# Borders between blocks of 768 tokens: preparation ahead of the last second products, weight remainders in halves, two PSUM banks exchanged in every second pair

## The chip, the cores and the metric

The kernel runs on one core of one Trainium2 chip, in one launch. The metric is device time in microseconds, from three runs before the change (median 1062.34, lowest 1061.27, highest 1062.95). A core has five engines with a queue of instructions each: PE (TensorE, matrix products; its weight loads are listed as PEld), DVE (VectorE), ACT (ScalarE), POOL (GpSimd) and SP, which here only issues DMA transfers. They run side by side and wait for each other by semaphores.

## The reference

The program chains three parts. An attention with a position bias gives 2304 tokens of 512 values. Two feed-forward layers follow, each with two products (512 to 2048 and 2048 to 512):

```python
def _moe_ref(x, w_in, w_out):
    h = x @ w_in
    g = h - np.tanh(h)
    return (g @ w_out).astype(np.float32)

def _moe2_ref(x, w_in, w_out, s, b):
    h = x @ w_in
    r = np.maximum(h, 0.0)
    g = s * (r * r) + b
    return (g @ w_out).astype(np.float32)
```

The change concerns the second of them (layer 1) alone.

## The kernel before

All products keep float32 accuracy by splitting a matrix into a rounded part and a remainder (`rounded`, `rest`, line 92); a product is then three matmuls: high by high, high by low, low by high.

The attention and the first layer come first, up to about 666 us. The second layer works on three blocks of 768 tokens (`SUPER`, the loop over `q`), one after the other. A block has three stages.

**Eight pairs.** The loop over `p` takes two of the 16 groups of hidden units at a time, for both halves (384 tokens) of the block. It uses a seven-product scheme in place of eight block products (a Strassen-Winograd scheme): `combine` (line 644) forms four sums of weight quarters on POOL in tile XB, and `part` (line 652) splits weights and sums into a rounded part (three copies on ACT) and a remainder (line 92, three subtractions on POOL), in tile `C0` or `C1` by turns. `product` (line 824) is six matmuls of 384 columns. A pair has seven products in four PSUM banks X, Y, Z, V: first X, Y, Z, V, then X, Z, V again. ACT and DVE add them up, apply the squared ReLU (`squashed`, L718, and `units`, L722) and, for the first half of the tokens, split the result with `upper` (L728, ACT) and `lower` (L734, DVE). For the second half the two results of each pair are kept whole in SBUF, as "held units". Between the products of a pair stand the second products of the pair before, for half 0 (`second_products`, line 582: per hidden group 3 token tiles with three matmuls of 512 columns).

**The border.** After the last pair the second products of half 0 for hidden groups 14 and 15 are due, then `leave` (L586) copies the three accumulated tiles out, one on DVE and two on ACT.

**Half 1.** For each of the 16 held units, `ahead(f)` allots two buffers of a ring of 11 (tag "bias") and calls `upper` and `lower`; `second_products(1, f)` then does nine matmuls with them into banks Z, V and a3. The ring is also used by `leave` and by the pairs.

In the same loop the next block's tokens are prepared: `tokens(q + 1)` returns 15 steps, kept in the list `xq`: two loads, then rounding copies on ACT (`hi`, L679) and remainders and differences on DVE (`lo`, L682, and `minus`, L685, both of them with two inputs from SBUF). Three steps are taken at the end of the last pair, the fourth behind the preparation of unit 1, the others one per unit. The last block has no successor: it has none of this, and leaves its last three units' products to be ordered by token tile.

The order of every engine's queue is the order of the program; there is no planner that reorders. Around the border the program has this order (lines 894 to 907):

```python
            ahead(0)
            second_products(0, NF - 2, pend.pop(0))
            ahead(1)
            if xq:
                xq.pop(0)()
            second_products(0, NF - 1, pend.pop(0))
            if not final:
                part(q + 1, 0)
                combine(q + 1, 1)
            late = 3 if final else 0
            for f in range(NF - late):
                ahead(f + 2)
                if xq:
                    xq.pop(0)()
                second_products(1, f, gs.pop(f))
```

The opening of a block is its first pair, `p` = 0, and the first four products of `p` = 1. In the first block the last second products of layer 0 lie between them (`fill`); in the other two blocks nothing does, so the eleven products follow each other directly.

Of the kernel before, what the change touches and what calls it, by code (L numbers as in the profile page):

```python
# [24 lines left out]
NF = DFF // 128  # L25
# [35 lines left out]
def tile_kernel(ctx, tc, qk, vd, wcat, wts, sb, ltab, psib, ipsi8, out):  # L61
# [8 lines left out]
    def place(tag, shape, dtype=F32):  # L70
        return pools[0 if tag in EARLY else 1].tile([128] + shape, dtype, tag=tag, name=tag)
# [19 lines left out]
    def rest(lo, raw, hi):  # L91
        nc.gpsimd.tensor_tensor(out=lo, in0=raw, in1=hi.bitcast(F32), op=ALU.subtract)  # L92
# [118 lines left out]
    with ExitStack() as c0:  # L211
# [40 lines left out]
        for n in range(NG + 2):  # L252
# [18 lines left out]
            if n < NG:  # L271
# [3 lines left out]
                f = 512 - y  # L275
# [23 lines left out]
    def ring(dtype):  # L299
        return bp.tile([128, S], dtype, tag="bias", name="ring")  # L300
# [59 lines left out]
    with ExitStack() as ca:  # L360
# [163 lines left out]
        for n in range(NK + 6):  # L524
# [30 lines left out]
            if n in TK:  # L555
                k, j = TK[n]
# [11 lines left out]
    with ExitStack() as cb:  # L568
# [5 lines left out]
        def accumulate(layer, o, w, gh, gl, d, first, last):  # L574
            if layer == 0:
                wh, wl_ = (w[:, l, d * 128:d * 128 + 128] for l in range(2))
                prods = ((wh, gh), (wh, gl), (wl_, gh))
            else:
                a, l = gh[:, d * 128:d * 128 + 128], gl[:, d * 128:d * 128 + 128]
                prods = ((a, w[:, 0]), (a, w[:, 1]), (l, w[:, 0]))  # L580
            for j, (x, y) in enumerate(prods):
                nc.tensor.matmul(o, x, y, start=first and j == 0, stop=last and j == 2)  # L582
# [63 lines left out]
        def part(q, p):  # L646
            w, sums_ = wf_t.pop((q, p)), sums_at.pop((q, p))
            cs = cs_t[q, p] = place(f"C{(p + q) % 2}", [7, 2, 256], F32R)
            groups = ((slice(4, 6), w[:, 0].rearrange("p (o n) -> p o n", o=2)), (slice(6, 7), w[:, 1:2, 256:512]),
                      (slice(0, 4), sums_))  # L650
            for o, x in groups:
                nc.scalar.copy(cs[:, o, 0], x)  # L652
            for o, x in groups:
                rest(cs[:, o, 1], x, cs[:, o, 0])

        def unit(u, i, l):
            k = (0, 4, 6, 2, 8, 10, 12)[u] + i
            tag, k0 = ("XA", 0) if k < 4 else ("C2", 4) if k < 9 else ("C3", 9)
            if tag not in unit_at:
                unit_at[tag] = place(tag, [4 if k0 == 0 else 5, 2, 384], F32R)  # L660
            return unit_at[tag][:, k - k0, l]
# [55 lines left out]
        def squashed(layer, c, t):  # L717
            nc.scalar.activation(out=t, in_=c, func=(AF.Tanh, AF.Relu)[layer])  # L718
# [29 lines left out]
        xq = tokens(0)  # L748
        for n in range(NS):
# [15 lines left out]
            c, f = seq[n]  # L765
# [33 lines left out]
        def bank(t, n=384):  # L799
            return (ps_a if t[0] == "a" else ps_g).tile([128, 512], F32, tag=t, name=t)[:, 0:n]  # L800

        fill = [lambda: gemm2(*seq[-2]), lambda: gemm2(*seq[-1])]
        for q, (layer, s_) in enumerate(SUPER):
            nd = 3 if layer else 4
            cols = 512 if layer else 384
            c0 = s_ * 768
            final = q == len(SUPER) - 1
            accs = {}
            g_at.clear()

            def second_products(half, f, gs):
                order = (["a0", "a1", "a2", "a3"], ["V", "Y", "Z", "X"] if not layer else ["Z", "V", "a3"])[half][:nd]
                for d in range(nd):
                    if f == 0:
                        accs[half, d] = bank(order[d], cols)
                    accumulate(layer, accs[half, d], wt[f, 1], *gs, d, f == 0, f == NF - 1)
                    if f == NF - 1:
                        leave(accs[half, d], layer, d, c0 + half * 384)

            def product(o, p, a, u, begins):  # L820
                cs = cs_t[q, p]
                for i in range(2):
                    for j, (l, r) in enumerate(((0, 0), (0, 1), (1, 0))):
                        nc.tensor.matmul(o, cs[:, a, l, i * 128:i * 128 + 128], unit(u, i, r),  # L824
                                         start=begins and i == 0 and j == 0, stop=i == 1 and j == 2,
                                         skip_group_check=not begins)

            pend = []
            for p in range(NF // 2):
                X, Y, Z, V = (bank(t) for t in "XYZV")  # L830
                load_w(q, p + 2)
                u2, r, t_x = (ring(F32)[:, 0:384] for _ in range(3))
                product(X, p, 4, 0, True)
                nc.scalar.copy(u2, X)
                if p + 1 < NF // 2:
                    part(q, p + 1)
                product(Y, p, 0, 1, True)
                nc.vector.tensor_tensor(out=u2, in0=Y, in1=u2, op=ALU.add)
                product(Z, p, 1, 2, True)
                nc.vector.tensor_tensor(out=r, in0=Z, in1=u2, op=ALU.add)  # L840
                product(V, p, 2, 3, True)
                nc.vector.tensor_tensor(out=Y, in0=V, in1=r, op=ALU.add)
                if pend:
                    second_products(0, 2 * p - 2, pend.pop(0))
                elif fill:
                    fill.pop(0)()
                squashed(layer, Y, r)
                units(layer, held_unit(2 * p + 1), Y, r)
                product(X, p, 5, 4, False)
                squashed(layer, X, t_x)  # L850
                units(layer, X, X, t_x)
                product(Z, p, 6, 5, False)
                nc.vector.tensor_tensor(out=Z, in0=Z, in1=u2, op=ALU.add)
                g1 = two()
                upper(layer, X, g1)
                t_z = ring(F32)[:, 0:384]
                squashed(layer, Z, t_z)
                lower(layer, X, g1)
                units(layer, Z, Z, t_z)
                product(V, p, 3, 6, False)  # L860
                nc.vector.tensor_tensor(out=V, in0=V, in1=u2, op=ALU.add)
                g2 = two()
                upper(layer, Z, g2)
                lower(layer, Z, g2)
                squashed(layer, V, t_z)
                units(layer, held_unit(2 * p), V, t_z)
                if pend:
                    second_products(0, 2 * p - 1, pend.pop(0))
                elif fill:
                    fill.pop(0)()  # L870
                pend = [g1, g2]
                if p + 1 < NF // 2:
                    combine(q, p + 2)
                if q == 0 and p == 0 and layer:
                    renewed(NF - 3)
                    for f in (NF - 2, NF - 1):
                        renew(f)
                if q == 0 and p == 1 and layer:
                    for f in (NF - 2, NF - 1):
                        renewed(f)  # L880

                if p == NF // 2 - 1 and not final:
                    xq = tokens(q + 1)
                    for _ in range(3):
                        xq.pop(0)()
            gs = {}

            def ahead(f):
                if f < NF:
                    gs[f] = two()  # L890
                    upper(layer, held_unit(f), gs[f])
                    lower(layer, held_unit(f), gs[f])

            ahead(0)
            second_products(0, NF - 2, pend.pop(0))
            ahead(1)
            if xq:
                xq.pop(0)()
            second_products(0, NF - 1, pend.pop(0))
            if not final:  # L900
                part(q + 1, 0)
                combine(q + 1, 1)
            late = 3 if final else 0
            for f in range(NF - late):
                ahead(f + 2)
                if xq:
                    xq.pop(0)()
                second_products(1, f, gs.pop(f))
            if late:
                ahead(NF - 1)  # L910
                for d in range(nd):
                    for f in range(NF - late, NF):
                        accumulate(layer, accs[1, d], wt[f, 1], *gs[f], d, False, f == NF - 1)
                    r0 = c0 + 384 + d * 128
                    o = ring(F32)[:, 0:512]
                    for h, copy, queue in ((slice(0, 256), nc.scalar.copy, nc.scalar), (slice(256, 512), nc.vector.tensor_copy, nc.sync)):
                        copy(o[:, h], accs[1, d][:, h])
                        queue.dma_start(out=out[r0:r0 + 128, h], in_=o[:, h])
# [57 lines left out]
```

## Time and profile before

| | us |
|---|---|
| median of three runs | 1062.34 |
| the profiled execution, its own time | 1059.94 |
| its span | 1058.2 |
| PE busy | 1042.2 |
| DVE busy | 626.9 |
| ACT busy | 535.3 |
| POOL busy | 459.7 |

The span runs from the first to the last instruction of one profiled execution; times within it are counted from its start. Rows of a timeline give a start, a duration, the engine, the line and operation, what is written and read, how many instructions are merged into the row, and in brackets the idle time just before with the instruction that ended it. Instructions of one engine overlap a little, so that the distance from start to start is shorter than a duration. In the kernel before, the first border's half 1 begins at 764.06 us and the second block's first pair at 800.06.

### The profile page before, as it was taken

What the parts mean: (1) busy time and instruction counts of PE and PEld (TensorE: products, weight loads), DVE (VectorE), ACT (ScalarE), POOL (GpSimd) and SP (SyncE); (2) the same over time, 40 slices, a digit from 0 to 9 for tenths busy, and PEclk for the clock granted to TensorE, in tenths of its full rate; (3) what the DMA queues carried; (4) which work ended last, traced back from release to release, by engine and by line L of the source; (5) the groups of instructions that cost most, each with busy time, mean ns of one, the idle gap of its engine ahead of it and who ended that gap; (6) DMA issues with size and microseconds to landing.
All of it is one profiled execution on the core that took longest, in us unless ns stands there. A gap on an engine that the chain in (4) does not pass through costs nothing.

```text
span 1058.2 us, 19045 instructions
## 1 busy us (share of the span) xinstructions
PE 1042.2 (98%) x7048; PEld 844.0 (80%) x7048; DVE 626.9 (59%) x1297; ACT 535.3 (51%) x1110; POOL 459.7 (43%) x630
## 2 busy tenths in 40 slices
PE   9999999999999999999999999999999999999998
PEld 6566666666688888899888888999878998799986
DVE  8888888888577555533544325555575556655552
ACT  8987787877465433323332334554444444444441
POOL 0067777787468312130131062575225662166500
PEclk9999999999999999999999999999999999999999
DMA  8957464542264164330542331311302122022000
GB/s 286 326 167 275 154 220 162 180 135 91 105 258 140 67 206 149 126 120 31 195 164 80 124 106 52 113 45 41 110 0 91 41 60 90 0 90 60 2 30 30
DMA packets 53772, 124.87 MB, mean 118 GB/s; under 512 B 6064, under 2 KB 12336, under 8 KB 53680
## 3 DMA queue, kind: packets, MB, share of 16 engines
q1 hardware_dynamic: 53248, 123.28, 34.8%
q8 instruction: 55, 0.90, 0.3%
q10 hardware_dynamic: 432, 0.39, 0.1%
q14 instruction: 37, 0.30, 0.1%
HBM read 90.19 MB, written 33.46 MB: 117 GB/s over the span
## 4 chain that ended last, share of the span: by engine, by line
PE 87%; DVE 4%; POOL 2%; ACT 1%; issue 1%; DVEq 0%; POOLq 0%; ACTq 0%
PE a L582 31%; PE h L340 19%; PE o L504 7%; PE s L405 6%; PE X L824 5%; PE V L824 5%; PE Z L824 5%; PE t L449 3%; PE Z L582 3%; PE V L582 2%; PE Y L824 2%; POOL pn L443 1%; DVE raw L412 1%; DVE XA L682 1%; PE c L449 1%
## 5 line engine op out<-in xcount | busy, mean ns | idle before, releaser
L582 PE MATMUL a<-ring,w 128*128 128x512 f32 (+1 forms) x960 | 210.3, 368 | 0.0
L582 PEld LDWEIGHTS a<-ring,w 128*128 128x128 f32 x960 | 168.4, 189 | 29.8
L443 POOL TENSOR_SCALAR pn<-p,sm 128x576 f32<-128x576 f32 (+2 forms) x224 | 131.7, 604 | 40.8 <-DVE sm L434 35.5
L582 PE MATMUL a<-w,ring 128*128 128x512 f32 x576 | 146.6, 392 | 0.0
L349 DVE TENSOR_TENSOR h<-h,ring 128x512 f32<-128x512 f32 (+1 forms) x80 | 51.7, 646 | 152.1 <-ACT ring L348 152.0
L348 ACT ACTIVATE ring<-h 128x512 f32<-128x512 f32 (+1 forms) x80 | 44.4, 555 | 187.0 <-PE h L340 187.0
L582 PEld LDWEIGHTS a<-w,ring 128*128 128x128 f32 x576 | 107.6, 188 | 20.5
L340 PE MATMUL h<-X,C 128*128 128x512 f32 (+1 forms) x576 | 118.3, 355 | 0.0
L92 POOL TENSOR_TENSOR C<-st,C 128x512 fp32r<-128x512 f32 (+1 forms) x48 | 47.9, 1020 | 159.2 <-ACT C L652 105.7
L412 DVE CUSTOM_DVE_ANT_0 raw<-s,bias 128x576 f32<-128x576 f32 x144 | 103.9, 753 | 19.0 <-PE s L405 14.5
L426 ACT ACTIVATE p<-raw,mn 128x576 f32<-128x576 f32 x144 | 110.9, 774 | 7.1 <-DVE mn L412 4.3
L340 PEld LDWEIGHTS h<-X,C 128*128 128x128 f32 x576 | 96.3, 189 | 16.3 <-issue 0.8
L504 PE MATMUL o<-pt,vv 128*64 128x256 f32 (+1 forms) x640 | 95.0, 418 | 1.3 <-DVE xo L511 1.3
L405 PE MATMUL s<-qk 64*128 64x288 f32 (+1 forms) x640 | 91.8, 430 | 1.7 <-DVE mn L412 1.3
L136 POOL TENSOR_SCALAR s<-st 128x512 f32<-128x512 f32 x36 | 23.3, 649 | 150.7 <-DMA st<-in_wts 115.0
L405 PEld LDWEIGHTS s<-qk 64*128 64x128 f32 (+1 forms) x640 | 47.0, 175 | 42.6 <-DVE mn L412 18.6
L357 DVE TENSOR_TENSOR ring<-h,ring 128x512 fp32r<-128x512 f32 (+1 forms) x80 | 50.9, 637 | 43.6 <-ACT ring L356 39.2
L340 PE MATMUL h<-XA,C 128*128 128x512 f32 x288 | 70.6, 390 | 0.0
L340 PEld LDWEIGHTS h<-XA,C 128*128 128x128 f32 x288 | 53.9, 188 | 11.0
L356 ACT CAST ring<-h 128x512 fp32r<-128x512 f32 (+1 forms) x80 | 43.5, 543 | 36.5 <-DVE h L349 36.5
L487 ACT COPY pt<-t 128x512 f32<-128x512 f32 x64 | 37.4, 584 | 43.8 <-PE c L449 26.9
L449 PEld LDWEIGHTS t<-ident,pn 64*128 64x128 f32 x1184 | 51.8, 139 | 9.6 <-DVE pt L487 1.5
(118 smaller groups left out, 1854.0 us busy)
## 6 DMA issues: line engine op xcount, KB each, us to landing
st<-in_wts SPq DMA_DIRECT2D x36, 512.0 KB, 3.7
w<-in_wts SPq DMA_DIRECT2D x28, 512.0 KB, 5.0
qk<-in_qk SPq DMA_DIRECT2D x16, 864.0 KB, 5.5
st<-w_d SPq DMA_DIRECT2D x24, 512.0 KB, 3.5
bias_d<-m SPq DMA_DIRECT2D x36, 296.0 KB, 4.6
bias<-bias_d SPq DMA_DIRECT2D x32, 288.0 KB, 4.2
w_d<-s SPq DMA_DIRECT2D x32, 256.0 KB, 2.1
vv<-in_vd SPq DMA_DIRECT2D x16, 320.0 KB, 3.7
```

The source lines that it names most:

```text
L92: nc.gpsimd.tensor_tensor(out=lo, in0=raw, in1=hi.bitcast(F32), op=ALU.subtract)
L340: nc.tensor.matmul(h, a, x, start=(k == 0), stop=(k == 3 * KD - 1))
L349: nc.vector.tensor_tensor(out=h, in0=h, in1=t, op=(ALU.subtract, ALU.mult)[layer])
L357: nc.vector.tensor_tensor(out=gl, in0=g, in1=gh.bitcast(F32), op=ALU.subtract)
L405: nc.tensor.matmul(o[0:n, c, 0:288], q[h, ee, t * 128:t * 128 + n], kk[h, ee], start=True, stop=True)
L412: nc.vector.tensor_tensor_reduce(out=raw.rearrange("p (c j) -> p c j", c=2), in0=s_t.pop((x, j))[:, :, 0:288], in1=bias_t[pairs[i][0], k]. ...
L426: nc.scalar.activation(out=p, in_=raw, func=AF.Exp, scale=-1.0, bias=mn, accum_out=sm[:, j:j + 1])
L443: nc.gpsimd.tensor_scalar(out=pn[:, c:c + b - a], in0=p[:, a:b], scalar1=sm[:, j:j + 1], scalar2=0.0, op0=ALU.mult, op1=ALU.add)
L449: nc.tensor.transpose(out_, in_, ident[ROWS[r], ROWS[r]])
L504: nc.tensor.matmul(o[h], v[:, e, j], unit_t[i, u][:, 8 if j == 4 else 4 * e + j, 0:n], start=(j == 0), stop=(j == 4))
L582: nc.tensor.matmul(o, x, y, start=first and j == 0, stop=last and j == 2)
L824: nc.tensor.matmul(o, cs[:, a, l, i * 128:i * 128 + 128], unit(u, i, r), start=begins and i == 0 and j == 0, stop=i == 1 and j == 2, skip_ ...
```

## The change

`part` no longer subtracts the four sums' remainders in one instruction of 1024 columns but in two of 512. In pairs with an odd number the names X and Y stand for each other's bank. At the border the order is new: unit 0, then `part` of the next block's first pair, then unit 1, the second products of group 14, unit 2, those of group 15, then `combine`. In half 1 the loop prepares unit f+3 instead of f+2, and the token steps begin with unit 1 instead of between units 1 and 2 of the preparation.

```diff
-            for o, x in groups:
+            for o, x in groups[:2]:
                 rest(cs[:, o, 1], x, cs[:, o, 0])
+            for k in (0, 2):
+                rest(cs[:, k:k + 2, 1], sums_[:, k:k + 2], cs[:, k:k + 2, 0])
...
-                X, Y, Z, V = (bank(t) for t in "XYZV")
+                X, Y, Z, V = (bank(t) for t in ("XYZV", "YXZV")[p % 2])
...
             ahead(0)
+            if not final:
+                part(q + 1, 0)
+            ahead(1)
             second_products(0, NF - 2, pend.pop(0))
-            ahead(1)
-            if xq:
-                xq.pop(0)()
+            ahead(2)
             second_products(0, NF - 1, pend.pop(0))
             if not final:
-                part(q + 1, 0)
                 combine(q + 1, 1)
             late = 3 if final else 0
             for f in range(NF - late):
-                ahead(f + 2)
-                if xq:
+                ahead(f + 3)
+                if f and xq:
                     xq.pop(0)()
                 second_products(1, f, gs.pop(f))
             if late:
-                ahead(NF - 1)
```

## Rows read from the trace of the kernel before

**Rows 1.** The page, part 1: busy us, share of the span, instructions

```profile
PE 1042.2 (98%) x7048; PEld 844.0 (80%) x7048; DVE 626.9 (59%) x1297; ACT 535.3 (51%) x1110; POOL 459.7 (43%) x630
```

**Rows 2.** The waits of PE from 600 us on: us in total, times, longest

```profile
PE Z L582 <- ACT ring L728: 4.6, 2, 2.3
PE X L824 <- DVE ring L734: 1.0, 2, 0.5
```

**Rows 3.** Stages (length; PE, PEld, DVE, ACT, POOL busy; clock; DMA): border, opening, border

```profile
757.90:800.06 42.16, 39.82 (x173) 31.78 (x172) 26.58 (x45) 19.09 (x39) 8.21 (x7) 1.00 0.05 19
800.06:812.32 12.26, 11.74 (x68) 11.42 (x67) 7.86 (x14) 7.52 (x15) 9.01 (x9) 1.00 0.48 152
...
886.50:928.66 42.16, 39.79 (x173) 31.79 (x172) 26.59 (x45) 19.09 (x39) 8.21 (x7) 1.00 0.05 20
```

**Rows 4.** Timeline of PE, last border: its first group and its last

```profile
1015.10 6.32 PE L582 MATMUL a<-w,ring 128*128 128x512 f32 x27
...
1051.86 2.20 PE L582 MATMUL a<-w,ring 128*128 128x512 f32 x9
```

**Rows 5.** Timeline of PE, first border: half 1's start and its unit 3

```profile
764.06 0.84 PE L582 MATMUL Z<-w,ring 128*128 128x512 f32 x3
...
769.50 0.84 PE L582 MATMUL a<-w,ring 128*128 128x512 f32 x3
772.62 1.15 PE L582 MATMUL Z<-w,ring 128*128 128x512 f32 x3 [2.29 <-ACT ring L728]
```

**Rows 6.** Timeline of ACT, first border

```profile
760.73 1.12 ACT L728 ACTIVATE ring<-X,sb_t 128x384 fp32r<-128x384 f32 x2
...
764.74 0.93 ACT L652 CAST C<-st 128x512 fp32r<-128x512 f32 x2
765.57 1.05 ACT L652 CAST C<-XB 128x1024 fp32r<-128x1024 f32 x1
766.51 0.62 ACT L728 ACTIVATE ring<-X,sb_t 128x384 fp32r<-128x384 f32 x1
...
771.54 0.51 ACT L679 CAST XA<-C 128x384 fp32r<-128x384 f32 x1 [4.01 <-DVE C L685]
771.96 1.12 ACT L728 ACTIVATE ring<-X,sb_t 128x384 fp32r<-128x384 f32 x2
```

**Rows 7.** Timeline of DVE, first border

```profile
761.38 1.15 DVE L734 SCALAR_TENSOR_TENSOR ring<-X,sb_t,ring 128x384 fp32r<-128x384 f32 x2 [0.62 <-ACT ring L728]
762.44 0.55 DVE L682 TENSOR_TENSOR XA<-C,XA 128x384 fp32r<-128x384 f32 x1
...
767.77 2.74 DVE L682 TENSOR_TENSOR XA<-C,XA 128x384 fp32r<-128x384 f32 x1
...
775.15 1.02 DVE L685 TENSOR_TENSOR C<-C 128x384 f32<-128x384 f32 x2
777.26 0.62 DVE L734 SCALAR_TENSOR_TENSOR ring<-X,sb_t,ring 128x384 fp32r<-128x384 f32 x1 [1.10 <-ACT ring L728]
```

**Rows 8.** Timeline of POOL, first border

```profile
765.44 2.00 POOL L92 TENSOR_TENSOR C<-st,C 128x512 fp32r<-128x512 f32 x2 [18.74 <-ACT C L652]
767.39 2.71 POOL L92 TENSOR_TENSOR C<-XB,C 128x1024 fp32r<-128x1024 f32 x1
770.17 0.92 POOL L644 TENSOR_TENSOR XB<-st 128x256 f32<-128x256 f32 x1
```

**Rows 9.** Timeline of PE, opening of the second block: first products of its second pair

```profile
808.04 1.31 PE L824 MATMUL X<-XA,C 128*128 128x384 f32 x6 [0.52 <-DVE ring L734]
809.20 1.20 PE L824 MATMUL Y<-C,C 128*128 128x384 f32 x6
810.24 1.20 PE L824 MATMUL Z<-C,C 128*128 128x384 f32 x6
```

**Rows 10.** Timeline of DVE, opening of the second block: the two lowers

```profile
807.37 0.62 DVE L734 SCALAR_TENSOR_TENSOR ring<-X,sb_t,ring 128x384 fp32r<-128x384 f32 x1 [0.19 <-ACT ring L728]
...
809.18 0.62 DVE L734 SCALAR_TENSOR_TENSOR ring<-Z,sb_t,ring 128x384 fp32r<-128x384 f32 x1 [0.19 <-ACT ring L728]
```

## Prediction

> **What bounds the kernel now.** I read the busy times first: PE is busy for 98% of the span and no other engine for more than 59% [rows 1]. So a gain must be a gap on PE, and a delay elsewhere costs only if PE comes to wait for it. PE's list of waits shows, for the part that the change touches, two waits of Z for ACT's L728 (together 4.6 us) and two of X for DVE's L734 (together 1.0) [rows 2]. The table of stages places them: the passage from one 768-token block to the next takes 42.16 us, once in each of the two inner borders, and the opening of a block 12.26 [rows 3]. The granted clock is 1.00 in all of them, the higher of its two levels (2.4 GHz), so no clock is in play.
>
> The last border is the measure of an undisturbed passage, since no tokens of a next block are prepared there. From 1015.10 to 1051.86 PE starts 162 matmuls (27, then 135), 0.2269 us each [rows 4]. An inner border has 171: 38.80 us. It takes 42.16, so **3.36 us are lost per border**. They lie behind the third unit of the second half: half 1 begins at 764.06, one unit takes 2.04 us (nine matmuls), and unit 3, due at 770.18, starts at 772.62 after 2.29 us idle [rows 5]; the rest is a second, shorter stop at unit 5 and slow restarts.
>
> Why unit 3 is late stands on the other engines. The loop asks for unit f+2 (upper on ACT, then lower on DVE) before unit f's products, so only units 0 to 2 are under way when half 1 begins. ACT then does the three weight copies of the next block (L652, 764.74 to 766.51) before upper of unit 2; afterwards it stands still for 4.01 us until DVE has finished L685, whose result L679 rounds; upper of unit 3 starts only at 771.96 [rows 6]. DVE was late because its L682 at 767.77 lasted 2.74 us, where lower starts and ends within 0.62 [rows 7]: POOL was in its 1024-column subtraction, 767.39 for 2.71 us, until 770.10 [rows 8].
>
> **The change part by part.**
>
> *Order and lead at the border.* Removed: the three L652 copies between the evacuation of half 0 and unit 2. Added: two more units prepared ahead, with one token step fewer in front. Instruction by instruction it is the same work, except for one more POOL subtraction per weight pair. No DMA is issued by a moved step: the weight loads and the token loads keep their places on SP's queue, and the evacuation's DMAs go out about 0.6 us later with nothing waiting for them soon.
>
> ACT: upper of unit 0 runs at 760.73 and the next instruction can start 0.52 later [rows 6]. The copies then take the same 1.77 us (766.51 less 764.74), so upper of unit 1 starts near 763.0 and of unit 2 near 763.5. Behind these wait the two ACT evacuations of half 0 (about half a microsecond each) and upper of unit 3, near 765.1 to 765.7. Due times: unit 1 at 766.10, unit 2 at 768.14, unit 3 at 770.18. Unit 4 takes the ring buffers of unit 0, free when unit 0's products end at 766.10; due at 772.22. The copies cannot be held up: their weight tile is free when the last product ends at 757.90, and POOL had finished the sums long before (it was idle 18.74 us in front [rows 8]).
>
> DVE: lower follows upper, and its result is only needed by the third of each trio of matmuls, some 0.45 us after the unit's start. POOL started 0.70 us after the first copy (764.74, 765.44), so it now starts near 761.95. Its run is 2.00 + 2.71 + four additions at up to 0.92, 8.39 us: until 770.3, over lower of units 1 to 4 and the first token step, where today it lies over the second and later steps. What these then cost is not in the trace, so I bound it. Lower bound: no waiting, and lower of unit 5 starts when unit 1's ring buffers are free and upper is done, near 768.8. Upper bound: strict turns, each of the six DVE instructions in that stretch (0.55 each) added to POOL's 8.39: 761.95 + 8.39 + 3.30 = 773.6. I take 771, nearer the middle, because the 0.92 already contains waits for DVE and because DVE's waits overlap POOL's starts.
>
> From there a unit that comes with two subtractions and two ACT roundings needs 2.64 us (775.15 to 777.26 is 2.11 between the first subtraction and the next lower, plus 0.53 for a lower [rows 7]); such steps come at units 6, 8 and 11, the ones between need about 1.5, so over a pair they keep up with PE's 4.08. Lower of unit 6 would start at 771 + 2.64 = 773.6, and has time until 776.30 + 0.45 - 0.62 = 776.1. With the upper bound it is 776.2, 0.1 late. **So the whole 3.36 us go, 3.1 if the worst turns hold.** The token steps end one or two units later than now, with products of the next block starting only at 796.7.
>
> *Splitting the subtraction of the sums.* 512 + 256 columns take 2.00 us, so 512 cost at most 1.33 and two halves 2.67, against 2.71 for the whole [rows 8]. Zero for POOL, in all pairs of blocks; POOL is busy 43% [rows 1]. Its worth is that a blocked DVE instruction waits at most 1.3 us instead of 2.7, which stands in the bounds above.
>
> *Swapping two banks.* In the second pair of a block the first product now goes to the bank that was read early in the pair before. Today PE idles 0.52 us for L734, which ends at 807.37 + 0.62 = 807.99, and starts at 808.04 [rows 9, 10]. Eleven products at 1.04 (809.20 to 810.24) would take 11.44 and some hundredths, say 11.48; the stage takes 12.26, so 0.78 is lost. After the swap the first product starts at 807.36, the second at 808.42 finds lower of X done at 807.99, but the third, due at 809.46, writes Z, which the other L734 reads until 809.18 + 0.62 = 809.80 [rows 10]. A wait of 0.4 takes the place of the old one: Z starts near 809.85 instead of 810.24, and with a slow restart either way I take **0.3 us** per opening. Bounds: 0 (the wait moves wholly) and 0.78. It happens twice: in the first block an earlier block's products lie between. In all other pairs two groups of second products cover the waits already, and the swap costs nothing; without them it would be this same wait for Z.
>
> **The sum:** 2 x 3.36 + 2 x 0.3 = 7.3 us. The profiled execution took 1059.94 us with a span of 1058.2: it would become 1052.6. The median of the three runs is 1062.34, 2.4 above it; these are PE stalls that every run has, so I take them off the median: **1055.0**. About 0.2% (2.1 us) is what a measurement of this kernel can tell from no change.
>
> **The rivals.**
>
> *The wait comes back a few units later (14%).* What the trace shows for it is that L682 next to POOL's long subtraction took 2.74 us [rows 7, 8], and POOL's whole run now lies just where the lead is being built up. If one such block of about 2.2 us (2.74 less 0.55) is still on the chain to unit 6 or 8 in each border, the gain shrinks by up to 4.4: 1059.4. By the halves it should be less; 1057.5 in the middle. Against it: the margin of 2.5 us at my middle estimate. The Trainium skill (SBUF — State Buffer, section Who interferes with whom) says a DVE instruction with two SBUF inputs contends with a GpSimd instruction that reads SBUF and that the later one is blocked wholly; the 2.74 agrees, and by that rule the lowers, which read two SBUF tiles too, are hit as L682 was, which is the upper bound above or this rival.
>
> *POOL does not let DVE in between (5%), and the kernel is slower.* Place: lower of unit 1, ready at 763.7, behind POOL's run. If it waited for all of it, until 770.3, it would end at 770.95, where unit 1's third matmul was due at 766.55: a stall of 4.4 in place of 3.36, 1.04 more per border, less 0.6 from the openings: 1063.8. It decides once POOL keeps DVE out past 769.6 (a loss then of more than today's). Against it: L682 ended at 770.51, just 0.41 behind POOL's end, and POOL's next instruction at 770.17 was stretched to 0.92; DVE did get in at the change of instruction [rows 7, 8].
>
> *Lead is not what is missing (5%).* If the slow units (2.64 against 2.04) followed each other the lead would be eaten and the same 2 to 3 us lost, only later: about 1061 to 1062, no change. Against it: today no stop follows unit 5 although the lead there is smaller.
>
> **How the numbers follow.** The forecast has 76%, the rivals 14, 5 and 5. Forecast and first rival are faster by over 0.2% (1059.4 is 2.9 below): 90%. Same 5%, slower 5%. The range begins at the largest gain, 2 x (3.36 + 0.78) = 8.3, 1054.0, less 0.8 for the scatter of runs; it ends beyond the middle of the first rival, at 1058.5. Left out are that rival's worst half and the two others.
>
> **What would show it.** Right: half 1 of an inner border runs without a stop at units 3 and 5; the stage is near 38.8 us; ACT has the three L652 copies directly behind upper of unit 0; POOL's run starts near 762; the opening takes about 11.9 with the wait at Z instead of X. Wrong: PE idle in front of L582 at units 5 to 8, an L734 of over 2 us at the border, or a wait of PE in the other pairs of a block.

## The result, and the profile after

The changed kernel takes 1052.97 us (median of 4 runs, 1052.11 to 1053.19) against 1062.09 (4 runs, 1061.27 to 1062.95): a ratio of 0.9913, 95% interval 0.9895 to 0.993. It is 9.1 us faster. The forecast was faster by 7.3, at 1055.0; the measured time lies 0.23 us below the range given.

The profiled execution took 1053.08 us with a span of 1051.3. In its table of stages (length; PE, PEld, DVE, ACT, POOL busy; granted clock; DMA share; GB/s) the rows are the first passage, the opening after it, the second passage and its opening; they answer to [rows 3].

```profile
758.70:797.50 38.80, 38.80 (x172) 32.09 (x172) 26.77 (x45) 19.21 (x39) 9.02 (x8) 1.00 0.06 21
797.50:809.50 12.00, 11.76 (x68) 11.44 (x66) 7.76 (x14) 7.41 (x15) 8.88 (x10) 1.00 0.50 154
883.68:922.49 38.81, 38.81 (x173) 32.10 (x172) 26.79 (x45) 19.22 (x39) 9.05 (x8) 1.00 0.06 21
922.49:934.49 12.00, 11.77 (x68) 11.45 (x67) 7.76 (x14) 7.41 (x15) 8.90 (x10) 1.00 0.44 153
```

A passage took 42.16 us and takes 38.80, with PE busy all the time; an opening took 12.26 and takes 12.00. Over both borders that is 2 x 3.36 + 2 x 0.26 = 7.24 us. The two waits of [rows 2] are gone from PE's list. In their place stands one of 0.2 us each, at Z of the opening, for the L734 that is L736 now:

```profile
PE Z L826 <- DVE ring L736: 0.5, 2, 0.2
```

ACT at the first border, to set beside [rows 6]. The half begins 0.80 us later in this trace than in that of before (764.86 against 764.06), because everything ahead of the blocks ended 0.80 later; all starts below are to be read with that shift.

```profile
761.53 0.62 ACT L730 ACTIVATE ring<-X,sb_t 128x384 fp32r<-128x384 f32 x1
762.05 0.92 ACT L652 CAST C<-st 128x512 fp32r<-128x512 f32 x2
762.86 1.05 ACT L652 CAST C<-XB 128x1024 fp32r<-128x1024 f32 x1
763.82 1.12 ACT L730 ACTIVATE ring<-X,sb_t 128x384 fp32r<-128x384 f32 x2
764.84 1.05 ACT L586 COPY ring<-a 128x512 f32<-128x512 f32 x2
765.78 0.62 ACT L730 ACTIVATE ring<-X,sb_t 128x384 fp32r<-128x384 f32 x1
```

DVE there, beside [rows 7]: lower of units 1 and 2, of units 3 and 4, the first token step's remainder, and lower of units 5 and 6.

```profile
764.46 2.25 DVE L736 SCALAR_TENSOR_TENSOR ring<-X,sb_t,ring 128x384 fp32r<-128x384 f32 x2 [1.67 <-ACT ring L730]
...
767.24 2.06 DVE L736 SCALAR_TENSOR_TENSOR ring<-X,sb_t,ring 128x384 fp32r<-128x384 f32 x2
769.22 1.08 DVE L684 TENSOR_TENSOR XA<-C,XA 128x384 fp32r<-128x384 f32 x1
...
771.24 1.09 DVE L736 SCALAR_TENSOR_TENSOR ring<-X,sb_t,ring 128x384 fp32r<-128x384 f32 x1
...
774.49 0.62 DVE L736 SCALAR_TENSOR_TENSOR ring<-X,sb_t,ring 128x384 fp32r<-128x384 f32 x1 [1.10 <-ACT ring L730]
```

POOL there, beside [rows 8]:

```profile
762.73 1.99 POOL L92 TENSOR_TENSOR C<-st,C 128x512 fp32r<-128x512 f32 x2 [15.09 <-ACT C L652]
764.69 3.17 POOL L92 TENSOR_TENSOR C<-XB,C 128x512 fp32r<-128x512 f32 x2
...
770.86 1.05 POOL L644 TENSOR_TENSOR XB<-st,XB 128x256 f32<-128x256 f32 x1
```

A pair of lowers took 1.15 us before; beside POOL's run the two pairs take 2.25 and 2.06 (the longest single lower 1.65), and POOL's two halves 3.17. The delay is there; PE does not feel it, since the result of the lower of unit 5, which starts at 771.24, is needed only at 775.06 + 0.45.

So the removed gaps are all in place, and yet 1.9 of the 9.1 us (9.1 less 7.24) have no gap that would explain them. That was the question for the runs.

### The profile page after: what moved, and what is told of

It is laid out like the page before. It is cut to its first block, busy times and chain, and to the rows that moved or that the text cites. A ratio compares the mean times of both kernels' runs of the same rounds, so it can differ in the third digit from the quotient of the medians.

```text
span 1051.3 us, 19063 instructions
## 1 busy us (share of the span) xinstructions
PE 1040.4 (99%) x7048; PEld 844.4 (80%) x7048; DVE 626.9 (60%) x1297; ACT 535.4 (51%) x1110; POOL 464.6 (44%) x654
## 4 chain that ended last, share of the span: by engine, by line
PE 91%; DVE 3%; DMA 2%; ACT 1%; issue 1%; POOL 1%; SPq 0%; DVEq 0%; ACTq 0%
PE a L582 31%; PE h L340 19%; PE o L504 7%; PE s L405 6%; PE Z L826 5%; PE V L826 5%; PE Y L826 3%; PE X L826 3%; PE V L582 3%; PE Z L582 3%; PE t L449 3%; PE b L284 2%; DMA bias_d<-m 1%; DVE raw L412 1%; DMA qk<-in_qk 1%
## 5 line engine op out<-in xcount | busy, mean ns | idle before, releaser
L92 POOL TENSOR_TENSOR C<-XB,C 128x512 fp32r<-128x512 f32 x48 | 62.5, 1324 | 0.0
```

## The experiments

Each stands beside runs of the kernel before on the same chip. First came the kernel before itself and the change's parts.

**The kernel before, unchanged**

> The kernel before, unchanged, for its trace. The measured gain, 9.1 us, is 1.8 more than the sum of the PE gaps, 7.24 in the traces (two passages from 42.16 to 38.80 us, two openings from 12.26 to 12.00). Theory A: the change saves those 7.24 us and nothing else; the rest is scatter of the part ahead of the blocks, since the profiled execution of before was 2 us shorter than its other runs. Then this trace reaches the first product of the blocks later than the 666.67 us of the first trace, by 0.5 to 2.5 us, and the passages and openings are again 42.16 and 12.26. Theory B: the change also shortens something outside the borders. Then this trace starts the blocks at 666.7 within 0.3, and the other stages explain nothing.

Measured: 1062.38 us (11 runs, 1060.46 to 1063.18), ratio 1.0 (0.9991 to 1.0009). Its blocks start at 667.35, 0.68 later than in the first trace, and its first passage takes 42.17. Its second does not take 42.16. In the table of stages the two passages and the 4.6 us after the stop in the second, then 2 us inside those:

```profile
758.57:800.74 42.17, 39.78 (x172) 31.76 (x172) 26.59 (x45) 19.11 (x39) 8.22 (x7) 1.00 0.05 19
887.18:930.35 43.17, 40.88 (x172) 33.09 (x172) 26.67 (x45) 19.21 (x39) 8.22 (x7) 0.96 0.05 19
901.91:906.55 4.64, 4.64 (x13) 3.44 (x13) 3.54 (x7) 2.00 (x5) 1.19 (x2) 0.63 0.01 2
...
904.00:906.00 2.00, 2.00 (x6) 1.61 (x5) 1.45 (x3) 0.99 (x3) 0.00 (x0) 0.50 0.01 4
```

and PE's timeline behind that stop:

```profile
901.91 1.40 PE L582 MATMUL Z<-w,ring 128*128 128x512 f32 x3 [2.29 <-ACT ring L728]
903.11 1.48 PE L582 MATMUL V<-w,ring 128*128 128x512 f32 x3
904.39 1.48 PE L582 MATMUL a<-w,ring 128*128 128x512 f32 x3
905.67 1.04 PE L582 MATMUL Z<-w,ring 128*128 128x512 f32 x3
906.55 0.85 PE L582 MATMUL V<-w,ring 128*128 128x512 f32 x3
```

Behind PE's stop of 2.29 us the granted clock is at 0.50, the lower level (1.2 GHz); three matmuls start 1.28 us after the three ahead of them instead of 0.68; then the clock is back. This passage is 1.00 us longer than the first, where the same stop was followed by a clock of 1.00. (The twelve matmuls from 901.91 to 906.55 take 4.64 us, where four groups at 0.68 and some 0.3 for the restart would make 3.0. The passage lost 1.00 and not 1.6, because the second stop, at unit 5, which with its restart costs 0.6 in the first passage, is missing here: the slower PE gave ACT and DVE time.) The shift of the start agrees with theory A, but the passage does not, and it is no effect of the change outside the borders, as B had it. I formed **theory C**: the clock falls behind the long stop in most executions, and the first trace of before happened to be one without.

**The change without the exchange of banks**

```diff
-                X, Y, Z, V = (bank(t) for t in ("XYZV", "YXZV")[p % 2])
+                X, Y, Z, V = (bank(t) for t in "XYZV")
```

> The change without the exchange of two banks. Theory A: passages 38.80, openings 12.26 with PE's wait of 0.5 us at X again; 0.5 us slower than the whole change, 6.7 us faster than before. Theory B, if the exchange is what brings the rest: 2 us or more slower than the whole change.

Measured: 1053.13 us (4 runs), ratio 0.9916 (0.9902 to 0.9929). Passages 38.80, openings 12.25 and 12.27. The exchange brings none of the 1.9 us.

**The exchange alone** (the same line, in the kernel before)

> The exchange of the two banks alone. Theory A: passages 42.16, openings 12.00 with a wait at Z in place of X; 0.5 us faster than before, too little to be told by the times, so the stages decide. Theory B, if the exchange brings the rest: about 2 us faster.

Measured: 1061.19 us (11 runs), ratio 0.9995 (0.9986 to 1.0004). Openings 11.97 and 11.98, with PE's wait of 0.23 us now at Z; the clock fell in both passages, 43.18 and 43.22.

**Order and lead alone** (the change without the halves and without the exchange)

> The new order at the border and the lead of three units, with the sums' remainders in one subtraction of 1024 columns and no exchange of banks. Theory A: lower of unit 2 is held up to about 767.5 (2.7 us behind the long subtraction) but due at 768.6, so the passage is still 38.80 to 39.1 and the time 6.1 to 6.7 us under before. Rival: the halves are needed; then a stop of 0.5 to 2 us at units 2 to 6, passage 39.3 to 40.8.

Measured: 1053.51 us (4 runs, 1053.05 to 1054.24), ratio 0.992 (0.9906 to 0.9934), passages 38.80. DVE's two lowers beside the undivided subtraction took 3.35 us together, one of them 2.75 alone, and still nothing stopped. The halves are not needed for this order.

The next four take the order apart, and one goes further.

**The halves alone** (the hunk in `part`, in the kernel before)

> The two halves of the sums' remainders alone, at the old order. The subtraction that lasted 2.74 us is now let in after the first half, some 1.3 us sooner, but the next one meets the second half. PE's stop at unit 3 should shrink from 2.29 to between 0.9 and 1.6 us, the passage from 42.16 to about 41. Theory C (the clock of PE falls behind a stop of 2.29 us, in some executions, and costs some 1.6 us each time; this is what the median of before holds beyond its first trace): falls become rarer or vanish with the shorter stop, so the runs lie at 1057 to 1060 with a mean clock of 0.999 to 1.000. Rival: the falls have nothing to do with the stop; then clocks of 0.997 and 0.998 appear here as in the kernel before.

Measured: 1060.32 us (10 runs, 1059.8 to 1060.93), ratio 0.9982 (0.9973 to 0.9991). PE's timeline at unit 3:

```profile
771.85 1.53 PE L582 MATMUL Z<-w,ring 128*128 128x512 f32 x3 [1.75 <-ACT ring L730]
```

and DVE's token step beside the halves:

```profile
767.53 1.64 DVE L684 TENSOR_TENSOR XA<-C,XA 128x384 fp32r<-128x384 f32 x1
769.20 1.53 DVE L687 TENSOR_TENSOR C<-C 128x384 f32<-128x384 f32 x1
```

The two instructions that took 2.74 and 0.96 us before take 1.64 and 1.53: the first is let in sooner, the second now meets the other half. That is 0.53 us less together, and the stop shrank by 0.54, to 1.75 us. In this trace the clock fell in both passages (42.70 and 42.71). Over the ten runs the recorded mean clock was 0.997 or 0.998 five times and 1.000 five times, but the times do not follow it (1059.98 to 1060.93 and 1059.80 to 1060.47); so what a fall costs behind this stop, or whether the record misses some, stays open.

**The weights' rounding ahead alone**

```diff
             ahead(0)
+            if not final:
+                part(q + 1, 0)
             second_products(0, NF - 2, pend.pop(0))
...
             if not final:
-                part(q + 1, 0)
                 combine(q + 1, 1)
```

> Only the weights' rounding of the next block is taken in front of unit 1; lead of two units, token steps and the long subtraction as before. ACT's upper of unit 2 comes 1.4 us sooner, but the first token step now meets the long subtraction (about 764.5 to 767.0) and the chain from it to upper of unit 3 ends near 771.5 where 770.5 is needed: a stop of 0.5 to 1.5 us at unit 3, passage 39.5 to 41.5. If theory C holds, mean clock 0.999 to 1.000 and a time near 1056 to 1059.

Measured: 1058.93 us (10 runs, 1057.77 to 1060.0), ratio 0.9973 (0.9963 to 0.9982), passages 41.42 and 41.43. There are two shorter stops in place of one:

```profile
769.08 0.50 PE L582 MATMUL Z<-w,ring 128*128 128x512 f32 x1 [1.02 <-DVE ring L734]
...
771.73 1.16 PE L582 MATMUL Z<-w,ring 128*128 128x512 f32 x3 [0.77 <-ACT ring L728]
```

No run has a mean clock below 0.999.

**The lead alone** (`part` back behind the second products of group 15, the subtraction whole)

> Only the lead of three units (with the token steps begun one unit later); the weights' rounding stays behind the second products of group 15, the subtraction stays whole. Theory D (lead is the whole cure): lower of unit 4 is held to about 770.6 by the long subtraction but due at 772.7, upper of unit 6 ends near 774.7 with 776.3 needed, so no stop and a passage of 38.8; about 1053.5. Rival: both the lead and the earlier rounding are needed; then a stop of 0.3 to 1.5 us at units 4 to 6, passage 39.1 to 40.5, 1054 to 1057.

Measured: 1054.36 us (4 runs, 1053.11 to 1055.24), ratio 0.9927 (0.9912 to 0.9942), passages 39.15 and 39.13. This is the lowest end of the rival's range. What is left is one small stop at unit 6, in PE's weight loads:

```profile
777.56 0.30 PEld L582 LDWEIGHTS Z<-w,ring 128*128 128x128 f32 x2 [0.23 <-ACT ring L728]
778.22 0.19 PEld L582 LDWEIGHTS Z<-w,ring 128*128 128x128 f32 x1 [0.35 <-DVE ring L734]
```

Lead is nearly the whole cure, 3.0 of 3.36 us; the earlier rounding brings the last 0.35, by starting ACT's copies, and POOL's run behind them, 3.5 us sooner (762.05 against a half that begins at 764.86; here 766.03 against 765.35).

**The whole change, with a third bank**

```diff
+                if q and p == 1:
+                    Z = bank("a3")
```

> The whole change, and in the second pair of blocks two and three Z stands in the free bank a3, so that its first product need not wait for lower of Z. If that wait (0.24 us with a slow restart, 0.5 us per opening against 11.48) is all that is left of the opening, the openings take 11.5 instead of 12.0 and the kernel gains 1.0 us on the whole change: 1052.0. If V's product then waits for the last units instead, it gains 0 to 0.5.

Measured: 1051.44 us (4 runs, 1051.34 to 1052.18), ratio 0.9902 (0.9887 to 0.9917). Passage and opening:

```profile
758.85:797.65 38.80, 38.80 (x173) 32.10 (x172) 26.75 (x45) 19.22 (x39) 9.01 (x8) 1.00 0.06 21
797.65:809.12 11.47, 11.47 (x67) 11.42 (x66) 7.77 (x14) 7.23 (x15) 8.36 (x9) 1.00 0.47 161
```

The wait at Z was all that was left; the opening is now 0.53 us shorter than with the exchange of X and Y alone. This is the fastest kernel of the study, though its interval overlaps that of the whole change: the 1.06 us are shown by the stages, not by the times.

The last four, on one chip, were for theory C.

**The whole change, again**

> The whole change again, next to the three that follow. Theory C (falls of PE's clock come behind long stops of PE): no stop over 0.3 us is left at the borders, so every run has a mean clock of 0.999 or 1.000 and the scatter is about 1 us: 1052 to 1053.5.

Measured: 1052.68 us (5 runs, 1051.63 to 1053.7), ratio 0.9911 (0.9897 to 0.9925); mean clock 1.000 in every run. The scatter is 2.1 us and not 1, without any fall.

**Lead, exchange and third bank**

> The lead of three units, the exchange of X and Y and bank a3 for Z in the second pair; the weights' rounding stays behind the second products of group 15 and the subtraction whole. If the earlier rounding and the halves only move margins, passages are 38.80 and openings 11.48, and the time is that of the best kernel so far, 1051.4 to 1052, 1 us under the whole change. Rival: the held-up token steps now end late and a stop comes back in the second half; passage 39 or more, 1053 to 1056.

Measured: 1053.34 us (5 runs, 1052.37 to 1054.03), ratio 0.9919 (0.9905 to 0.9933). Passages 39.14 and openings 11.49 and 11.47: the 0.34 of the lead alone stay. The expected 38.80 was wrong here and the rival right, with passage and time inside its ranges: the earlier rounding does more than move a margin.

**An artificial stop in the changed kernel**

```diff
-                ahead(f + 3)
+                if final or f not in (7, 10):
+                    ahead(f + 3)
+                elif f == 10:
+                    for _ in range(3):
+                        upper(layer, held_unit(9), g9)
+                    ahead(10)
+                    ahead(13)
...
+                g9 = gs.pop(f)
-                second_products(1, f, gs.pop(f))
+                second_products(1, f, g9)
```

> The whole change with an artificial stop in half 1 of both inner borders: unit 10 is prepared only after ACT has rewritten unit 9's rounded buffer three times, which waits for unit 9's last matmul. PE should stop about 2.2 us at unit 10, far from POOL's run and DVE's token chain of the border. Theory C: the clock falls behind it in most runs, mean clock 0.997 or 0.998, and each border costs 2.5 us of stop and restart plus about 1.6 us of slow clock: 1058 without, 1059.5 to 1061.5 with falls. Rival (the falls come from something else in the old border, not from the length of the stop): clock 1.000 in all runs and 1057.5 to 1058.5.

Measured: 1061.14 us (11 runs, 1059.52 to 1062.59), ratio 0.999 (0.9981 to 0.9999). The stop at unit 10, and the passage with the 4.6 us behind the stop:

```profile
788.41 1.45 PE L582 MATMUL Z<-w,ring 128*128 128x512 f32 x3 [2.34 <-ACT ring L730]
```

```profile
759.35:802.57 43.22, 40.88 (x172) 33.14 (x172) 26.95 (x45) 21.03 (x42) 9.04 (x8) 0.96 0.05 19
788.41:793.00 4.59, 4.59 (x12) 3.48 (x13) 4.45 (x9) 3.12 (x7) 0.00 (x0) 0.63 0.00 0
```

Nearly the whole gain is gone, with nothing but a stop that stands far from POOL's run. All 11 runs have a mean clock of 0.996 to 0.998. A mean clock of 0.998 stands for one fall and less for two: in the second trace of before, 4.64 us at 0.63 lower the mean over 1059.8 us by 0.0016, and that trace has 0.998; this kernel's trace, with a fall in both passages, has 0.997. The four runs with 0.998 take 1059.52 to 1059.95, the seven lower ones 1060.52 to 1062.59, so one more fall costs about 1.9 us here, where no second stop gives part of it back.

**The same, shorter** (`range(1)`)

> The same with one rewriting in place of three: a stop of about 1.2 us at unit 10. Theory C, with stops of 0.8 to 1.0 us seen without falls and one of 1.75 with falls in half the runs: no falls, clock 0.999 to 1.000, 1.5 us per border, 1055.5 to 1056.5. Rival: falls as behind the long stop.

Measured: 1055.44 us (5 runs, 1055.08 to 1055.76), ratio 0.9939 (0.9926 to 0.9952).

```profile
785.79 1.16 PE L582 MATMUL Z<-w,ring 128*128 128x512 f32 x3 [1.04 <-ACT ring L730]
```

```profile
758.02:798.37 40.35, 39.31 (x172) 31.96 (x172) 26.85 (x45) 19.81 (x40) 9.02 (x8) 1.00 0.06 21
```

Mean clock 1.000 in all runs. The 1.04 us of stop cost 1.55 per passage, 0.51 of it for the slow restart. With the same restart the long stop of 2.34 would cost 2.85; it cost 4.42 (43.22 less 38.80). The 1.57 that remain are the price of the slow clock; the 1.9 above hold the runs' scatter as well.

Together, by the longest stop of PE at the border or in the opening behind it, as each kernel's trace shows it:

| longest stop, us | kernels | runs with a mean clock of 0.998 or less |
|---|---|---|
| 2.29 to 2.34 | before, exchange alone, long stop | 81 of 87 |
| 1.75 | halves alone | 5 of 10 |
| 1.02 to 1.04 | rounding ahead alone, short stop | 0 of 15 |
| 0.52 or less | the change (twice) and the five others | 0 of 30 |

All runs with a clock on record are in it, except the first trace of before, which has no fall. The halves alone ran on another chip than the long stop and the exchange alone; on that chip the kernel before fell in 15 of 19 runs, so the step from 2.29 to 1.75 us is less sure than that to 1.04, behind which no run fell.

## Why the prediction was right in its parts and wrong in its number

**The border's gap.** Right: 38.80 us were named, 38.80 and 38.81 measured. The walk through the queues holds too, after the shift of 0.80: upper of unit 1 near 763.0 (763.02), of unit 3 near 765.1 (764.98), POOL from 761.95 (761.93), lower of unit 5 near 771 (770.44), of unit 6 near 773.6 (773.69). The bounds of 768.8 and 773.6 for unit 5 were needed: DVE and POOL did hold each other up there. The Trainium skill (SBUF — State Buffer, section Who interferes with whom) says that a DVE instruction with two SBUF inputs contends with a GpSimd instruction that reads SBUF; the lowers of 2.25 and 2.06 a pair agree. The lower of unit 6, which was to decide the rival "the wait comes back", was not late, so that rival did not come about.

One premise was wrong and cost nothing: that nothing waits soon for the DMAs of the evacuation. At the second border ACT's upper of unit 5 waits for one of them, since it takes a ring buffer that the DMA has to empty first; PE reaches unit 5 only at 900.05.

```profile
894.54 0.62 ACT L730 ACTIVATE ring<-X,sb_t 128x384 fp32r<-128x384 f32 x1 [2.06 <-DMA out_x<-ring]
```

**The parts' shares.** The forecast did not say which part carries the gain. The lead does (39.15 without the rest); the earlier rounding closes the last 0.35, and alone leaves 41.42. The halves were put at "Zero for POOL", with a worth that "stands in the bounds above": POOL's pair of halves takes 2.55 us in an opening of the changed kernel, where one subtraction took 2.42, and 3.17 against 2.71 at the border. They did shorten the longest single lower, from 2.75 to 1.65 us (the forecast had a wait of at most 1.3), but passages are 38.80 with and without them. They are a margin that nothing used.

**The openings.** Right in mechanism, 0.26 against 0.3: the wait moved from X to Z. The third bank shows that the wait was the rest.

**What failed** is the step "The granted clock is 1.00 in all of them, the higher of its two levels (2.4 GHz), so no clock is in play", and with it "these are PE stalls that every run has, so I take them off the median". Every run has the stalls, but in most a fall of the clock comes behind them, and the one trace that was read had none: its execution, at 1059.94, lay 2.4 us below the median, and that was put down as an offset that stays. Most of it was falls. Over the 65 runs of the kernel before in the experiments, the 6 with a mean clock of 1.000 have a median of 1060.5 us, the 18 with 0.998 (one fall) 1061.5, the 41 below (two) 1062.5: 1.0 us for each fall, as in the trace (43.17 against 42.17). The groups overlap: one run at 1.000 took 1062.56, and the start of the blocks scatters as well. The sum made whole is 7.24 + 2 x 1.0 = 9.2 us, and 9.1 were measured. From the runs without a fall, 1060.5, the changed kernel is 7.5 us away: there the forecast of 7.3 holds. The term that was missing is the price of a stop beyond its own length; the range had only 0.8 us for scatter on that side, which was 0.23 too little.

**The rivals.** The one on the slower side did not come about: POOL let DVE in about once per instruction, as the row of before had suggested. "Lead is not what is missing" was refuted by the lead alone.

Three things stay open: why the same stop of 2.29 us is followed by a fall in one passage and not in another; what a fall costs behind the stop of 1.75 us; and the scatter of up to 2.2 us that is left in kernels without any fall. The blocks begin between 665.98 and 668.12 us in the traces, whatever the kernel; no run looked for the cause.

## What to carry to other kernels

A gap on the engine that sets the end can cost more than its length: look at the granted clock of several runs, and when the profiled execution is faster than all the others, ask what the others have that it has not, before its offset is carried along. When a unit's preparation arrives late now and then, try more lead first, as long as buffers last: here it brought 3.0 of 3.36 us, and rearranging the work that delays the unit brought the rest. A wait that is removed by giving a result another bank can move to the next bank in line, as it did here from X to Z, so count that one as well.

## What the runs showed of the hardware that was not expected

PE's clock fell to its lower level, 0.50 in the 2 us looked at, behind single stops of 2.3 us in the midst of work that was otherwise nearly without a gap, and was back at the higher one some 4 us after the restart. It did so in most runs, not behind every such stop; behind stops of about 1 us it did not fall in 15 runs. While POOL had one instruction after another to run, DVE's instructions with two SBUF inputs came through about one per POOL instruction (two lowers 2.25 us instead of 1.15); lowers with one input from PSUM kept their 0.62 beside POOL in the opening of the changed kernel.
